# One pair of VectorE instructions for the row sums of both heads in an attention + mixture-of-experts kernel

## The chip, the cores and the metric

The kernel runs on one core of a Trainium2 chip. The metric is the device time of one execution in microseconds (us); lower is better. Before the change it is 1745.02 us, the median of three runs (1744.03 to 1747.92).

## The reference

Attention with a learned relative-position bias over 4 batches, 8 heads, 576 tokens and a head width of 64, and behind it eight dense experts (512 to 1024 to 512) over the 2304 tokens, each weighted by a gate that is normalised eight times over rows and columns. What the change touches is the softmax:

```python
scores = scale * np.matmul(q, k.transpose(0, 1, 3, 2))
...
scores = scores + bias.transpose(2, 0, 1)[None, :, :, :]
scores = scores - np.max(scores, axis=-1, keepdims=True)
attn = np.exp(scores)
attn = attn / (np.sum(attn, axis=-1, keepdims=True) + 1e-09)
return np.matmul(attn, v).astype(np.float32)
```

The experts then compute `out += P[:, e:e+1] * (np.maximum(x @ w1[e], 0) @ w2[e])` for each of the eight.

## The kernel before

A **unit** is one batch and two heads; there are 16. The 576 query rows of a head lie in tiles: four of 128 rows, and one in which the last 64 rows of both heads stand together. A **step** handles two tiles of one head (group `gi` 0 or 1, head `hh` 0 or 1) or the one shared tile (`gi` 2), so a unit has five steps: two pairs, of head 0 and head 1 over the same tokens, and a single one; 80 steps in all. For each tile of a step:

- TensorE multiplies the scores into a PSUM tile `s` (two of them).
- VectorE adds the bias and takes the row's extreme in one instruction (`st_max`, shown as CUSTOM_DVE_ANT_0 in the trace and ISA in the order, followed by a read of the accumulator); it writes the tile `sb` (six buffers) and a column of the statistics tile `st`.
- ScalarE takes the exponential in place, and the row sum with it (`st_exp`, followed by ACTIVATION_READ_ACCUMULATOR).
- VectorE adds 1e-9 to the sums and scales them (TENSOR_SCALAR), then takes the RECIPROCAL: `st_rcp`, one pair of instructions for each step.
- ScalarE multiplies the tile by the reciprocal into the high 16-bit half of `ah` (`st_hi`), and VectorE makes the low half from the rest (`st_lo`). `ah` has two buffers; in units 4 to 11 every third step uses a piece of `xc` as a third.
- A DMA transpose, issued from SyncE's queue, turns both halves into `aT` (three buffers for the steps with two tiles).
- Two steps later in program order `attend` multiplies by V, both heads of a pair in one group of 28 matmuls into `pv`.

While attention runs, TensorE also does the first expert, for blocks of tokens whose attention is finished ("pieces": `l<-xa`, `l<-xb`, `l<-xc` is its first layer, `l<-area` with 512 columns its second). They fill the gaps between scores and `pv`. The first units overlap with the computation of the bias and with the scaling of the first expert's weights.

The order on each engine is not the order of the code. A planner (`Plan`) records every operation with a cost, finds what depends on what from the memory regions, and picks for each engine, in simulated time, the ready operation of the highest priority and lowest number. A changed dependence or a changed place in the code can therefore move instructions all over the attention stage. Engines then run their lists strictly in order. The expert stage behind it (from 500 us on) has a planner run of its own.

The lines that matter:

```python
for n in range(NS + LAG + 1):
    ...
    if 0 < n <= NS:
        st_rcp(steps[n - 1])
    ...  # scores of step n + 1
    if n < NS:
        st_exp(steps[n])
    if n + 1 < NS:
        st_max(steps[n + 1])
    ...  # attend what is due
    if 0 < n <= NS:
        st_hi(s)      # s = steps[n - 1]
        st_lo(s)
```

Calls through the planner all have the line L210 in the trace, so the rows are told apart by their tiles.

Of the kernel before, what the change touches and what calls it, by code (L numbers as in the profile page):

```python
# [10 lines left out]
F32 = mybir.dt.float32  # L11
# [7 lines left out]
P = 128  # L19
# [251 lines left out]
def attention_sinkhorn_moe(ctx, tc, q, k, v, w1, b1, w2, wg, m1, m2, xm, xm4, xf, sel, out):  # L271
# [141 lines left out]
    with ExitStack() as actx:  # L413
# [4 lines left out]
        def places(name, bufs=1, space=None):  # L418
            kw = {} if space is None else {"space": space}
            p = atc.enter_context(tc.tile_pool(name=name, bufs=1, **kw))  # L420
            return Places(lambda k, n, size: p.tile([n, size], F32, name=k), bufs)
# [13 lines left out]
        nat, spl, uni, bst, wrk = places("nat", 4), places("spl"), places("uni", 2), places("bst", 2), places("wrk")  # L435
# [187 lines left out]
        def bias_step(between=()):  # L623

            i = bpos[0]
            bpos[0] += 1
            if between:
                if 0 < i <= NBLK:
                    bias_back(i - 1)
                for j, fn in enumerate(between):  # L630
                    fn()
                    if j == 0 and i < NBLK:
                        bias_front(i)
                return
            if i < NBLK:
                bias_front(i)
            if 0 < i <= NBLK:
                bias_back(i - 1)
# [145 lines left out]
        def b_tile(u, t, hh):  # L784
            if t in (2, 3):
                return U[u]["b", hh][:, t - 2, :]
            hp = units[u][1]
            return br[t][:, 2 * hp + hh, :] if t < 2 else br4[:, hp, :]
# [68 lines left out]
        def flush(n):  # L857
            while len(evacs) > n:
                evacs.pop(0)()
# [51 lines left out]
        def st_scores(s):  # L911
            u, gi, hh = s["key"]
            s["ps"] = []

            def one(t):
                with plan.as_one():
                    s["ps"].append(scores(u, t, hh))

            return [lambda t=t: one(t) for t in s["ts"]]

        def st_max(s):
            u, gi, hh = s["key"]
            st = wrk.tile([P, 4, 2], F32, name="st", tag="st", bufs=5)
            s["st"], s["sb"] = st, []
            for i, t in enumerate(s["ts"]):
                sb = wrk.tile([P, S], F32, name="sb", tag="sb", bufs=6)
                s["sb"].append(sb)
                vec.tensor_tensor_reduce(
                    out=sb,
                    in0=s["ps"][i][:, :S],  # L930
                    in1=b_tile(u, t, hh),
                    scale=nc8[:, 0:1],
                    scalar=3.0e38,
                    op0=ALU.add,
                    op1=ALU.min,
                    accum_out=st[:, 0, i : i + 1],
                )

        def st_exp(s):
            st = s["st"]  # L940
            for i, sb in enumerate(s["sb"]):
                act.activation(
                    sb, sb, AF.Exp, scale=-1.0, bias=st[:, 0, i : i + 1], accum_out=st[:, 2, i : i + 1]
                )

        def st_rcp(s):
            st, n = s["st"], len(s["ts"])
            vec.tensor_scalar(
                out=st[:, 3, :n], in0=st[:, 2, :n], scalar1=EPS, scalar2=TM14, op0=ALU.add, op1=ALU.mult
            )  # L950
            vec.reciprocal(out=st[:, 3, :n], in_=st[:, 3, :n])
# [3 lines left out]
        def st_hi(s):  # L955

            n, u = len(s["sb"]), s["key"][0]
            if NHP <= u < 3 * NHP:
                ahs[0] += 1
            if ahs[0] % 3 == 2 and u < 3 * NHP:  # L960
                ah = xc[:, 1, : 4 * S].rearrange("p (i s) -> p i s", i=2)
            else:
                ah = wrk.tile([P, 2, 2 * S], F16, name="ah", tag="ah", bufs=2)
            s["ah"] = ah[:, :n]
            for i, sb in enumerate(s["sb"]):
                act.activation(s["ah"][:, i, 0:S], sb, AF.Copy, scale=s["st"][:, 3, i : i + 1])

        def st_lo(s):
            n, ah = len(s["sb"]), s["ah"]
            s["aT"] = wrk.tile([P, 9 * n, P], F16, name="aT", tag="aT" if n == 2 else "aT4", bufs=3 if n == 2 else 1)  # L970
            for i, sb in enumerate(s["sb"]):
                vec.scalar_tensor_tensor(
                    out=ah[:, i, S:],
                    in0=sb,
                    scalar=s["st"][:, 3, i : i + 1],
                    in1=ah[:, i, 0:S],
                    op0=ALU.mult,
                    op1=ALU.subtract,
                )
            sync.dma_start_transpose(out=s["aT"], in_=ah.rearrange("p n s -> p (n s)"))  # L980
# [85 lines left out]
        def w_stage(j):  # L1066
            if j == -4:
                sync.dma_start(out=wgt, in_=wg.rearrange("(a p) e -> p a e", p=P))
            if j in (-4, -3):
                w_load(0, j + 4)  # L1070
                w_max(0, j + 4)
            if j == 0:
                for i in (2, 3):
                    w_load(0, i)
                for i in (2, 3):
                    w_max(0, i)
                for i in range(4):
                    w_load(1, i)
            if j == 5:
                w_scale(0)  # L1080
                for i in range(4):
                    w_cut(0, i)
            if j == 6:
                for i in range(4):
                    w_max(1, i)
                w_scale(1)
                for i in range(4):
                    w_cut(1, i)
# [7 lines left out]
        steps = []  # L1096
# [7 lines left out]
        NS = len(steps)  # L1104
# [26 lines left out]
        for fn in st_scores(steps[0]):  # L1131
            fn()
        st_max(steps[0])
        def fill(n):
            while xevac:
                xevac.pop(0)()
            for _ in range(n):
                if bpos[0] <= NBLK:
                    bias_step()

        W0 = 6
        for n in range(NS + LAG + 1):
            while xevac:
                xevac.pop(0)()
            if 0 < n <= NS:
                st_rcp(steps[n - 1])
            if n < W0:
                bias_step(st_scores(steps[n + 1]))
            elif n + 1 < NS:
                for fn in st_scores(steps[n + 1]):  # L1150
                    fn()
            if n < NS:
                st_exp(steps[n])
            if n + 1 < NS:
                st_max(steps[n + 1])
            if n < W0:
                fill(1)
            flush(0)
            for d in [d for d in due if d[0] <= n]:
                due.remove(d)  # L1160
                attend(*d[1:])
            if 0 < n <= NS:
                s = steps[n - 1]
                st_hi(s)
                st_lo(s)
                u, gi, hh = s["key"]
                groups.setdefault((u, gi), []).append(s)
                if gi == 2 or hh == 1:
                    due.append((n + LAG, u, gi, groups.pop((u, gi))))
            if n < W0:  # L1170
                fill(2)
            for fn in hooks.get(n, ()):
                fn()
            if n == W0 - 1:
                assert bpos[0] > NBLK
                hpl = Places(lambda k, n, size: area[:, 8192:])
            w_stage(n - W0)
            for _ in range(2 if n % 5 in (0, 2, 4) or n < 20 else 1):
                if pieces and n >= 13:
                    run_piece(*pieces.pop(0))  # L1180
            if n % 5 == 0 and pieces and pieces[0][1] is None and pieces[0][2] % 2:
                run_piece(*pieces.pop(0))
# [165 lines left out]
    for t in range(0, NT, 8):  # L1348
        ts = range(t, min(t + 8, NT))
# [625 lines left out]
def _build(nc, arrays):  # L1975
    args = []
    for name, a in arrays.items():
        args.append(nc.dram_tensor(name, a.shape, mybir.dt.from_np(a.dtype), kind="ExternalInput").ap())
    args.append(nc.dram_tensor("out_0_dram", (N, DM), F32, kind="ExternalOutput").ap())
    with tile.TileContext(nc) as tc:  # L1980
        attention_sinkhorn_moe(tc, *args)
# [14 lines left out]
```

## Time and profile before

| | |
|---|---|
| median of three runs | 1745.02 us |
| the profiled execution | 1748.49 us |
| its span, first to last instruction | 1746.7 us |
| attention stage | up to about 500 us |
| TensorE busy over the span | 1670.3 us (96%) |
| VectorE busy | 1437.3 us (82%) |
| ScalarE busy | 1073.4 us (61%) |

Busy shares over the whole span mix two stages. Behind 500 us the experts run, and TensorE is busy almost without a break. Ahead of it, all of the engines and the DMA queue are busy for some 85 to 95% of the time, and which one is waited for changes from stretch to stretch; so the stretches are read one by one. [...]

### The profile page before, as it was taken

The numbers are of one execution on the slowest core, as the hardware profiler recorded it, in microseconds if no ns is written. First come the engines' busy times: TensorE is split into PE (matmuls) and PEld (weight loads), VectorE is DVE, ScalarE is ACT, GpSimd is POOL, SyncE is SP. The second block draws the span as 40 slices with busy tenths as digits, with TensorE's granted clock in tenths as the row PEclk, the third lists the DMA queues.
The fourth block names the chain that finished last, engine by engine and source line by source line (L and its number), as shares of the span: only waits on it lengthen the run. The fifth ranks groups of instructions, "written<-read, shape, count | busy, mean of one in ns | idle before, by whom it ended". The sixth has DMA issues, their size and how long they took to land.

```text
span 1746.7 us, 40339 instructions
## 1 busy us (share of the span) xinstructions
PE 1670.3 (96%) x16596; PEld 1369.6 (78%) x16596; DVE 1437.3 (82%) x2619; ACT 1073.4 (61%) x1912; POOL 98.4 (6%) x137
## 2 busy tenths in 40 slices
PE   7887897989999999999999999999999999999998
PEld 4554564656575888888988898889888888888887
DVE  6898989888879999778878887988788878876666
ACT  7897888888867556446455545555554644443443
POOL 0012011111102310100000000000000000000000
PEclk9997899999999999999999999999999999999999
DMA  7869899999986346734564456456544743462321
GB/s 251 257 174 230 184 213 206 212 195 204 187 242 212 136 153 239 254 138 164 198 249 157 165 199 217 170 181 221 209 165 166 268 167 130 178 227 100 102 76 37
DMA packets 291965, 324.61 MB, mean 186 GB/s; under 512 B 183100, under 2 KB 217412, under 8 KB 286788
## 3 DMA queue, kind: packets, MB, share of 16 engines
q1 hardware_dynamic: 291780, 322.04, 61.3%
q8 instruction: 129, 2.11, 0.5%
q14 instruction: 56, 0.46, 0.1%
HBM read 191.43 MB, written 88.08 MB: 160 GB/s over the span
## 4 chain that ended last, share of the span: by engine, by line
PE 81%; DVE 9%; DMA 4%; ACT 3%; issue 2%; POOL 0%; SPq 0%; DVEq 0%; ACTq 0%; POOLq 0%
PE bankA L1607 18%; PE bankA L1627 14%; PE bankE L1627 9%; PE bankB L1627 9%; PE bankE L1607 9%; PE l L210 8%; PE bankB L1607 4%; PE s L210 4%; PE pv L210 3%; DMA aT<-ah 2%; ACT area L210 2%; DVE area L210 1%; DVE ah L210 1%; DVE sb L210 1%; PE bankB L374 1%
## 5 line engine op out<-in xcount | busy, mean ns | idle before, releaser
L1607 PEld LDWEIGHTS <-slot 128*128 128x128 f16 x5040 | 450.9, 98 | 51.2 <-issue 5.3
L1627 PEld LDWEIGHTS <-hA 128*128 128x128 f16 x2268 | 221.1, 98 | 26.5 <-DVE hA L1219 1.2
L210 PEld LDWEIGHTS <-area 128*128 128x128 f16 (+1 forms) x2477 | 154.7, 100 | 101.6 <-issue 33.3
L1607 PE MATMUL bankA<-xt,slot 128*128 128x256 f16 (+1 forms) x1680 | 186.1, 262 | 0.7 <-ACT u L1664 0.7
L1607 PE MATMUL bankE<-xt,slot 128*128 128x256 f16 (+1 forms) x1680 | 186.1, 262 | 0.3 <-DVE c L1219 0.3
L1652 ACT ACTIVATE hA<-c 128x512 f16<-128x512 f32 x189 | 118.3, 628 | 108.7 <-DVE c L1219 107.7
L1627 PEld LDWEIGHTS <-hS 128*128 128x128 f16 x1512 | 147.5, 98 | 20.2 <-DVE hS L1658 1.9
L1627 PEld LDWEIGHTS <-area 128*128 128x128 f16 x1512 | 147.7, 98 | 17.1
L1711 ACT COPY u<-bankA 128x512 f32<-128x512 f32 (+1 forms) x70 | 37.9, 541 | 177.4 <-PE bankA L1627 177.2
L1219 DVE SCALAR_TENSOR_TENSOR hA<-c,hA 128x512 f16<-128x512 f32 x189 | 128.4, 691 | 16.1 <-ACT hA L1652 14.1
L1664 ACT ACTIVATE u<-bankA 128x512 f32<-128x512 f32 x126 | 75.2, 597 | 79.0 <-PE bankA L1607 72.2
L210 PE MATMUL l<-area 128*128 128x512 f16 (+1 forms) x413 | 112.1, 390 | 4.9 <-ACT area L210 1.7
L210 ACT ACTIVATE sb<-sb,st 128x576 f32<-128x576 f32 x144 | 110.7, 770 | 7.5 <-DVE st L210 7.3
L1219 DVE SCALAR_TENSOR_TENSOR acc<-c,fs,acc 128x256 f32<-128x256 f32 x252 | 110.4, 480 | 2.1
L210 DVE SCALAR_TENSOR_TENSOR ah<-sb,st,ah 128x576 f16<-128x576 f32 x121 | 97.8, 833 | 15.1 <-ACT ah L210 15.0
L210 PE MATMUL s<-qkT 128*128 128x512 f16 (+3 forms) x560 | 84.0, 300 | 13.8 <-DVE st L210 13.2
L210 ACT ACTIVATE ah<-sb,st 128x576 f16<-128x576 f32 x121 | 89.4, 771 | 10.5 <-DMA aT<-ah 6.9
L1627 PE MATMUL bankA<-area,hS 128*128 128x256 f16 x756 | 88.9, 273 | 1.8 <-ACT hS L1652 1.0
L1627 PE MATMUL bankA<-area,hA 128*128 128x256 f16 x756 | 88.4, 273 | 1.0 <-DVE hA L1219 1.0
L1627 PE MATMUL bankB<-area,hA 128*128 128x256 f16 x756 | 88.3, 273 | 0.0
L1627 PE MATMUL bankB<-area 128*128 128x256 f16 x756 | 88.3, 273 | 0.0
L1627 PE MATMUL bankA<-area 128*128 128x256 f16 x756 | 88.3, 273 | 0.0
(248 smaller groups left out, 3173.1 us busy)
## 6 DMA issues: line engine op xcount, KB each, us to landing
sc_w<-stage SPq DMA_DIRECT2D x84, 512.0 KB
acc<-sc_y SPq DMA_DIRECT2D x102, 256.0 KB
area<-sc_w SPq DMA_DIRECT2D x48, 512.0 KB
sc_y<-acc SPq DMA_DIRECT2D x84, 256.0 KB
xt<-sc_t SPq DMA_DIRECT2D x20, 1024.0 KB
slot<-sc_w SPq DMA_DIRECT2D x36, 512.0 KB
bt<-sc_bias SPq DMA_DIRECT2D x26, 576.0 KB
raw<-in_moe_w_dram SPq DMA_DIRECT2D x28, 512.0 KB
```

Source lines behind the costliest of these rows:

```text
L210: self.plan.record(self.name, cost, lambda: fn(*args, **kw), ins, outs, move)
L374: pe.matmul(ps, w[:, a, ft * P : (ft + 1) * P], xs(xp, dt, p0, W), start=(dt == 0 and j == 0), stop=(dt == 3 and j == 2),)
L1219: vec.scalar_tensor_tensor(out=o, in0=x, scalar=s, in1=y, op0=op0, op1=op1)
L1607: pe.matmul(ps[:, jf * w : jf * w + w], t[:, a, c * 512 + f * P : c * 512 + f * P + P], x(xp, c), start=(first and jf == 0 and c == 0 and ...
L1627: pe.matmul(ps[:, j * 256 : j * 256 + 256], h[:, a, fc * w + j * P : fc * w + j * P + P], t[:, wp, fc * 256 : fc * 256 + 256], start=(firs ...
L1652: on_act(0.58, lambda: act.activation(h[:, 0, sl], x, AF.Relu if relu else AF.Copy), [r], wk)
L1664: on_act(0.55, lambda: act.activation(tmp[k], bank[b], f, scale=HS), [b], [k], 0)
L1711: on_act(0.27 * nt, lambda: act.copy(tmp[k][:, :n], bank[b][:, :n]), [b], [k], 0)
```

## The change

Both heads of a pair now share one statistics tile of four columns (three buffers, where there were five of two columns). After the first head's step no TENSOR_SCALAR and RECIPROCAL are issued; after the second's one pair of them works on all four columns. The high and low halves of the first head are made only then, ahead of the next step's `st_max` in the code, because that one reuses the first head's `sb` tiles. The steps with the shared tile stay as they were. `EPS` is 1e-9, and `TM14` a power of two.

```diff
+        stq = [None]
+
         def st_max(s):
             u, gi, hh = s["key"]
-            st = wrk.tile([P, 4, 2], F32, name="st", tag="st", bufs=5)
-            s["st"], s["sb"] = st, []
+            if hh == 0:
+                stq[0] = wrk.tile([P, 4, 4], F32, name="st", tag="st", bufs=3)
+            s["stats"] = stq[0]
+            s["st"], s["sb"] = stq[0][:, :, 2 * hh : 2 * hh + 2], []
+            st = s["st"]
...
         def st_rcp(s):
-            st, n = s["st"], len(s["ts"])
+            st, n = s["stats"], 4 if s["key"][1] < 2 else 1
             vec.tensor_scalar(
                 out=st[:, 3, :n], in0=st[:, 2, :n], scalar1=EPS, scalar2=TM14, op0=ALU.add, op1=ALU.mult
             )
...
         for n in range(NS + LAG + 1):
             while xevac:
                 xevac.pop(0)()
-            if 0 < n <= NS:
+            ended = steps[n - 1]["key"] if 0 < n <= NS else None
+            waits = ended is not None and ended[1] < 2 and ended[2] == 0
+            if ended and not waits:
                 st_rcp(steps[n - 1])
...
             if n < NS:
                 st_exp(steps[n])
+            if ended and ended[2] == 1:
+                st_hi(steps[n - 2])
+                st_lo(steps[n - 2])
             if n + 1 < NS:
                 st_max(steps[n + 1])
...
             if 0 < n <= NS:
                 s = steps[n - 1]
-                st_hi(s)
-                st_lo(s)
+                if not waits:
+                    st_hi(s)
+                    st_lo(s)
```

**On VectorE**, in a late unit, before: `st_132` and `st_135` are the statistics of the two heads of a first pair, `st_139` and `st_143` those of the second pair; ISA is the score-plus-bias instruction into `sb`.

```order
L210 TENSOR_SCALAR st_132<-st_132 128x2
L210 ISA sb_134,st_139<-s_117,bt_122,sms 128x576
L210 ISA st_139 128x1
L210 RECIPROCAL st_132<-st_132 128x2
L210 SCALAR_TENSOR_TENSOR ah_144<-sb_136,st_146,ah_144 128x576
L210 TENSOR_TENSOR area<-l_1_115,area 128x512
L210 ISA sb_136,st_139<-s_119,bt_122,sms 128x576
...
L210 COPY qkT_127<-l_1_115 128x1024
L210 TENSOR_SCALAR st_135<-st_135 128x2
L210 RECIPROCAL st_135<-st_135 128x2
L210 SCALAR_TENSOR_TENSOR ah_142<-sb_137,st_132,ah_142 128x576
```

Now, at the same kind of place: `st_132` holds both heads of the first pair, `st_138` both of the second.

```order
L210 TENSOR_SCALAR st_132<-st_132 128x4
L210 RECIPROCAL st_132<-st_132 128x4
L210 SCALAR_TENSOR_TENSOR ah_141<-sb_136,st_132,ah_141 128x576
L210 SCALAR_TENSOR_TENSOR xc<-pv_112,xc 128x256
L210 ISA sb_136,st_138<-s_117,bt_124,sms 128x576
L210 ISA st_138 128x1
L210 SCALAR_TENSOR_TENSOR ah_141<-sb_139,st_132,ah_141 128x576
L210 SCALAR_TENSOR_TENSOR ah_142<-sb_140,st_132,ah_142 128x576
L210 ISA sb_139,st_138<-s_119,bt_124,sms 128x576
...
L210 SCALAR_TENSOR_TENSOR ah_142<-sb_133,st_132,ah_142 128x576
```

Before, the two heads' sums are treated apart, with the next pair's ISA between them; now one pair of instructions stands ahead of the low halves of both heads, and the ISA of the next pair's second head goes into an `sb` that the low half just before has set free.

**On ScalarE**, before (rows `sb<-sb` are exponentials, rows `ah<-sb` and `xc<-sb` high halves):

```order
L210 ACTIVATE ah_142<-sb_137,st_132 128x576
L210 ACTIVATE ah_142<-sb_140,st_132 128x576
L210 COPY qkT_127<-l_0_113 128x1024
L210 ACTIVATE sb_134,st_139<-sb_134,st_139 128x576
L210 ACTIVATE sb_136,st_139<-sb_136,st_139 128x576
L210 COPY qkT_127<-l_0_113 128x2x128
L210 ACTIVATE xb<-pv_112 128x256
L210 ACTIVATE xc<-sb_141,st_135 128x576
L210 ACTIVATE xc<-sb_133,st_135 128x576
```

And now, a little later in the list:

```order
L210 ACTIVATE sb_140,st_132<-sb_140,st_132 128x576
L210 ACTIVATE sb_133,st_132<-sb_133,st_132 128x576
L210 ACTIVATE qk_126<-nat_121,sms 128x9x64
L210 ACTIVATE sb_134,st_138<-sb_134,st_138 128x576
L210 ACTIVATE sb_135,st_138<-sb_135,st_138 128x576
L210 ACTIVATE ah_141<-sb_136,st_132 128x576
L210 ACTIVATE ah_141<-sb_139,st_132 128x576
L210 ACTIVATE xc<-sb_140,st_132 128x576
L210 ACTIVATE xc<-sb_133,st_132 128x576
```

Before, two high halves of one head alternate with exponentials; now the four of a pair stand in a row, behind the exponentials of the next step.

**On SyncE's queue**, before (`aT` is the transposed tile, `vnat`, `nat` and `bt` are loads for later units):

```order
L210 DMA_TRANSPOSE aT_125<-ah_144 128x18x128
L210 DMA nat_120<-in_k_dram 128x576
L210 DMA_TRANSPOSE aT_138<-ah_142 128x18x128
L210 DMA nat_121<-in_q_dram 128x576
L210 DMA_TRANSPOSE aT_0_118<-xc 128x9x128
L210 DMA bt_122<-sc_bias 128x1152
```

Now:

```order
L210 DMA nat_121<-in_q_dram 128x576
L210 DMA_TRANSPOSE aT_125<-ah_142 128x18x128
L210 DMA_TRANSPOSE aT_137<-ah_141 128x18x128
L210 DMA_TRANSPOSE aT_0_118<-xc 128x9x128
L210 DMA bt_122<-sc_bias 128x1152
```

The transposes of the two heads have moved together; the loads that stood between them stand ahead or behind.

## Rows read from the trace of the kernel before

**Rows 1.** Stretches: length, busy PE, PEld, DVE, ACT, POOL; PEclk, DMA share, GB/s.
```profile
100.00:150.00 50.00, 45.68 (x675) 28.90 (x674) 45.77 (x100) 46.45 (x93) 11.14 (x20) 1.00 0.78 192
150.00:205.00 55.00, 38.33 (x331) 22.59 (x329) 52.47 (x120) 41.45 (x79) 3.89 (x9) 0.75 1.02 230
205.00:275.00 70.00, 68.17 (x649) 43.20 (x644) 60.46 (x139) 59.31 (x121) 9.93 (x13) 0.98 0.96 201
275.00:310.00 35.00, 23.62 (x252) 14.20 (x252) 31.81 (x75) 28.19 (x59) 4.95 (x10) 0.82 0.94 203
310.00:500.00 190.00, 181.42 (x1821) 118.59 (x1820) 156.39 (x361) 156.28 (x321) 23.04 (x35) 0.98 0.97 201
```

**Rows 2.** Groups of TensorE, 275 to 310 us: busy us, mean ns | idle before, releaser.
```profile
L210 PE MATMUL pv<-aT,vs 128*64 128x256 f16 (+3 forms) x168 | 12.8, 298 | 3.4 <-DMA aT<-xc 2.3 <-DVE xb L210 0.6 <-DVE st L210 0.5
L210 PE MATMUL s<-qkT 128*128 128x512 f16 (+2 forms) x65 | 10.0, 296 | 5.2 <-DVE st L210 5.0
```

**Rows 3.** The same view, 310 to 345 us: the first expert's layer.
```profile
L210 PE MATMUL l<-xb,area 128*128 128x256 f16 x111 | 13.5, 273 | 0.0
```

**Rows 4.** Waits, 150 to 205 us: total us, times, longest.
```profile
PE s L210 <- DVE st L210: 8.5, 7, 2.6
PE pv L210 <- DMA aT<-ah: 4.0, 2, 2.3
```

**Rows 5.** Stretches of 5 us, columns as in rows 1.
```profile
280.00:285.00 5.00, 1.30 (x8) 0.54 (x7) 4.96 (x12) 5.00 (x11) 1.07 (x3) 0.85 0.85 157
285.00:290.00 5.00, 4.55 (x37) 3.02 (x38) 4.12 (x9) 1.85 (x5) 0.00 (x0) 0.50 0.96 221
```

**Rows 6.** Tile st, whole span: count, ns min/median/max, first and last start.
```profile
L210 DVE TENSOR_SCALAR st<-st x80: 131/159/506, 81.6 to 482.7; 128x2 f32<-128x2 f32 x64, 128x1 f32<-128x1 f32 x16
L210 DVE RECIPROCAL st<-st x80: 141/163/167, 83.5 to 482.9; 128x2 f32<-128x2 f32 x64, 128x1 f32<-128x1 f32 x16
```

**Rows 7.** Timeline of VectorE: start, us, operation.
```profile
333.72 0.17 DVE L210 TENSOR_SCALAR st<-st 128x2 f32<-128x2 f32 x1
333.79 0.81 DVE L210 CUSTOM_DVE_ANT_0 sb<-s,bt,sms 128x576 f32<-128x576 f32 x1
334.53 0.16 DVE L210 RECIPROCAL st<-st 128x2 f32<-128x2 f32 x1
334.61 0.80 DVE L210 SCALAR_TENSOR_TENSOR ah<-sb,st,ah 128x576 f16<-128x576 f32 x1
...
338.72 0.16 DVE L210 TENSOR_SCALAR st<-st 128x2 f32<-128x2 f32 x1
338.92 0.17 DVE L210 RECIPROCAL st<-st 128x2 f32<-128x2 f32 x1
339.00 1.54 DVE L210 SCALAR_TENSOR_TENSOR xc<-sb,st,xc 128x576 f16<-128x576 f32 x2
```

**Rows 8.** Tile st in 150 to 205, in 275 to 310 and in 310 to 500 us.
```profile
L210 DVE RECIPROCAL st<-st x10: 141/156/160, 154.6 to 202.9; 128x2 f32<-128x2 f32 x8, 128x1 f32<-128x1 f32 x2
...
L210 DVE RECIPROCAL st<-st x9: 151/160/167, 275.9 to 308.7; 128x2 f32<-128x2 f32 x7, 128x1 f32<-128x1 f32 x2
...
L210 DVE RECIPROCAL st<-st x40: 151/165/167, 313.3 to 482.9; 128x2 f32<-128x2 f32 x32, 128x1 f32<-128x1 f32 x8
```

**Rows 9.** Tile st, whole span: exponentials, high and low halves.
```profile
L210 ACT ACTIVATE sb<-sb,st x144: 758/767/837, 69.9 to 481.8; 128x576 f32<-128x576 f32 x144
L210 ACT ACTIVATION_READ_ACCUMULATOR sb<-sb,st x144: 185/191/263, 70.5 to 482.5; 128x1 f32 x144
L210 ACT ACTIVATE ah<-sb,st x121: 755/769/826, 85.9 to 489.6; 128x576 f16<-128x576 f32 x121
L210 DVE SCALAR_TENSOR_TENSOR ah<-sb,st,ah x121: 797/814/1254, 88.0 to 490.4; 128x576 f16<-128x576 f32 x121
```

**Rows 10.** Tile aT, 60 to 500 us: the transposes on SyncE's queue.
```profile
L210 SPq DMA_TRANSPOSE aT<-ah x67: 1271/3094/5702, 90.1 to 491.5; - x67
```

**Rows 11.** The chain of waits, 145 to 165 us: start, us, what.
```profile
152.40 8.72 DMA aT<-ah
```

## The prediction

> **What bounds the kernel now.** I began with the table of stretches [rows 1]. From 500 us on TensorE has hardly a gap and the change leaves that part's code as it is, so only the attention stage can move. In it two stretches differ from the rest. From 205 to 275 us TensorE is busy 68.2 of 70 us and from 310 to 500 us 181.4 of 190; from 150 to 205 us it is busy only 38.3 of 55 us at a mean clock of 0.75, and from 275 to 310 us 23.6 of 35 at 0.82. In these two VectorE is busy 52.5 of 55 and 31.8 of 35, the highest share of any compute engine: there it sets the pace.
>
> Next, the groups of TensorE in the second of them [rows 2]: before scores it stood idle 5.2 us (5.0 of it until VectorE had read the score tile), before `pv` 3.4 us, 2.3 of that for a transpose. The costly groups of the first expert that fill such gaps elsewhere (111 matmuls of one layer alone in the next 35 us, with 0.0 idle before them [rows 3]) are missing: no block was finished yet. From 150 to 205 us the waits say the same: 8.5 us of scores for VectorE, 4.0 us of `pv` for transposes [rows 4]. [...]
>
> [...]
>
> **The removed instructions.** There are 80 TENSOR_SCALAR and 80 RECIPROCAL on `st`, 64 of each on two columns [rows 6]. 64 heads make 32 pairs, so 32 of each go: 64 instructions. By their durations (medians 159 and 163 ns) that is 32 x 0.322 = 10.3 us. But the timeline shows that a duration is not what the queue gives up [rows 7]: a TENSOR_SCALAR starts at 333.72 and the next instruction 0.07 us later, a RECIPROCAL at 334.53 and its successor 0.08 later. Only where the RECIPROCAL directly follows and needs the result is it more: 338.72 to 338.92 to 339.00, 0.28 for both. In the order of instructions 37 of the 80 reciprocals directly follow their TENSOR_SCALAR before, and 26 of 48 now. So VectorE gives up 37 x 0.28 + 43 x 0.15 = 16.8 us before and 26 x 0.28 + 22 x 0.15 = 10.6 now: 6.2 us less, 0.19 per pair. Four columns have no row; two and one lie in one band (141 to 167 ns for the RECIPROCAL [rows 6]), so I cost four as two.
>
> [...]
>
> How much of it counts? Only pairs in the two stretches where VectorE sets the pace: 8 and 7 reciprocals on two columns [rows 8], one per head, so 7.5 pairs. 7.5 x 0.19 = 1.4 us. Where TensorE is full the cover is TensorE's own queue, and the gain there is nothing; without that cover it would be the other 24.5 x 0.19 = 4.7 us.
>
> **The added wait.** The one TENSOR_SCALAR now waits for the exponentials of the second head. Behind it on VectorE stand the RECIPROCAL, four low halves and the score instructions of the next pair's second head, which wait for `sb` tiles that these free; on ScalarE stand four high halves in a row. Is this loop too long? By [rows 7, 9]: the pair of instructions 0.36 us; two high halves and then the second low half, 0.77 + 0.77 + 0.81 = 2.35; two score instructions of 0.81 each, 1.62; the exponential and its read, 0.77 + 0.19 = 0.96. Sum 5.3 us a pair, without the handing over between engines. The pace is far slower: 32 two-column reciprocals in 190 us [rows 8] are 16 pairs, or 8 units of 23.8 us, and two loops are 10.6. So the six `sb` suffice and I cost this wait by itself at 0. If an engine's queue delays every turn of it by more than 6 us, that cover is gone.
>
> What is late next is `pv`. It needs both heads' transposes. The order shows them moved together: of 80 transposes 19 directly follow another one before, 37 now. SyncE's queue takes 3.09 us for one [rows 10]. The second head's low halves are done two low halves (1.5 us) after the first's, so its transpose stands for 3.09 - 1.5 = 1.6 us behind the first; and since its own high and low halves now come behind the first head's, another 1.5 us can be added. Bounds for one `pv`: 0 (what the planner puts in front covers it) to 3.1 us. Nor does a reason exclude a small gain: a load that stood between the two no longer delays the second one. No row here times that; I bound it by the shortest transpose, 1.3 us [rows 10]. Between -1.3 and 3.1 I take 1.6, the part that the queue itself forces.
>
> Where does it count? Where `pv` already waits for a transpose and nothing stands in front: twice from 150 to 205 us and once from 275 to 310 [rows 2, 4]. One of these is the transpose that took 8.72 us to land from 152.40 [rows 11]; that one was slow because of other traffic (the weights' loads), not for its neighbour, so I leave it out. 2 x 1.6 = 3.2 us. In the full stretches the first expert's matmuls cover it.
>
> **Sum.** -1.4 + 3.2 = +1.8 us. The profiled execution took 1748.49 us, 1.7 above its span and 3.5 above the median of 1745.02; with the same difference the median becomes about 1747.
>
> **Rivals.** *VectorE sets the pace all along, and fewer instructions are simply faster.* For it: its share is 95% and 91% in the slow stretches, and ScalarE and the DMA queue are not far behind TensorE elsewhere, so each unit may tighten. Against it: 0.0 idle of TensorE before the filling matmuls [rows 3], and a busy 95% there. Price: all 6.2 us by starts, which gives 1739; by durations 10.3, which gives 1735.
>
> *The late pair of transposes stops TensorE and drops its clock.* For it: the waits and the 0.50 behind the pause [rows 2, 4, 5]; two stretches in which nothing fills. Against it: the planner charges transfers and shifts `pv` accordingly. It decides once `pv` comes more than about 2 us later than what stands in front of it lasts. Price: three waits x 3.1 = 9.3 us, and one more stretch of 5 us at half clock, 2.5 us of lost work, less the 1.4 gained: +10.4, so 1755. With the clock lost at all three it is +15.4, so 1760.
>
> *It doesn't do what it says*: the planner only reshuffles, VectorE's saved time turns into VectorE's idle time and the transposes are covered. Then nothing moves: 1745.
>
> **How the numbers follow.** A measurement of this kernel can tell about 0.2%, 3.5 us, from no change. Forecast (1747, its own range 1742 to 1750): 0.35. Faster rival (up to 1741.5, around 1739): 0.32. Slower rival (from 1749, around 1755): 0.27. No effect (1745): 0.06. The forecast lies 0.29 within 3.5 us of the median and 0.06 above it. So faster 0.32, same 0.29 + 0.06 = 0.35, slower 0.06 + 0.27 = 0.33. The range leaves out a tenth on each side, about a third of either rival: what the faster one gives beyond its price by durations, and the slower one between its two prices and above: 1735 to 1758.
>
> **What would show it.** VectorE with 64 instructions fewer, 48 of each kind, four columns at about 160 ns; its busy time down by some 10 us but its place in the stage by less. Transposes in twos on SyncE's queue. The wait of `pv` for transposes, 6.3 us in the two slow stretches, up by about 3. The first expert stage starting within 4 us of 500. I am wrong if the waits for score tiles (8.5 and 5.0 us) shrink by more than 3 us, which is the faster rival, or if TensorE's clock in either slow stretch falls further, which is the slower one.

## The result, and the profile after

The changed kernel takes 1754.66 us (median of five; 1751.19 to 1754.94 without one disturbed execution of 8830.24 us) against 1745.02 before (median of five, 1742.55 to 1747.92): ratio 1.0051, 95% interval 1.0036 to 1.0066, so about 9 us slower. The range of the prediction, 1735 to 1758, holds it; its central 1747 does not. 1755 was the price of the rival in which the late pair of transposes stops TensorE.

The profiled execution of the changed kernel took 1751.19 us, the shortest of its runs, with a span of 1749.4; that of before (1748.49) was longer than any of those five runs, with a span of 1746.7. So the two profiles differ by 2.7 us only, and show less of the loss than the medians. The engines' row of the page: busy us, share, instructions.

```profile
PE 1671.4 (96%) x16596; PEld 1370.1 (78%) x16596; DVE 1428.4 (82%) x2555; ACT 1075.3 (61%) x1912; POOL 98.3 (6%) x137
```

VectorE has 64 instructions fewer (x2619 before) and 8.9 us less work (1437.3 before). Now the stretches of [rows 1], same columns, with the first half of the first one by itself in front:

```profile
100.00:125.00 25.00, 20.94 (x247) 12.40 (x244) 20.84 (x45) 19.30 (x38) 5.55 (x8) 0.88 0.80 190
...
150.00:205.00 55.00, 36.17 (x305) 21.87 (x303) 53.17 (x114) 42.32 (x78) 5.08 (x8) 0.78 0.96 234
...
275.00:310.00 35.00, 24.70 (x254) 14.56 (x252) 30.87 (x72) 31.64 (x66) 6.76 (x10) 0.90 1.09 221
310.00:500.00 190.00, 179.51 (x1789) 117.17 (x1790) 156.08 (x337) 157.96 (x320) 21.85 (x35) 0.98 0.98 203
```

The first 25 us of it before the change:

```profile
100.00:125.00 25.00, 21.75 (x288) 12.71 (x287) 24.40 (x56) 23.51 (x47) 4.77 (x8) 1.00 0.81 200
```

From 310 to 500 us VectorE's work hardly fell (156.39 before, 156.08 now), and TensorE does less (181.42, 179.51): work has moved to a later time. From 100 to 125 us, where the bias is made while the first heads run, VectorE had been busy 24.40 of 25 us and ScalarE 23.51. Now they are busy 20.84 and 19.30, and TensorE's granted clock (PEclk, as a share of full speed) is 0.88 there, where it was 1.00. This is a place that the prediction did not look at: it read 100 to 150 us as one row.

The tile `st` in the whole span now (count: ns min/median/max, first and last start):

```profile
L210 ACT ACTIVATE sb<-sb,st x144: 757/770/809, 68.4 to 484.1; 128x576 f32<-128x576 f32 x144
...
L210 DVE TENSOR_SCALAR st<-st x48: 109/158/259, 87.9 to 485.0; 128x4 f32<-128x4 f32 x32, 128x1 f32<-128x1 f32 x16
L210 DVE RECIPROCAL st<-st x48: 140/166/179, 88.3 to 485.2; 128x4 f32<-128x4 f32 x32, 128x1 f32<-128x1 f32 x16
...
who waited for it (us, times):
  DVE ah L210: 22.9, 21
...
  ACT sb L210: 16.7, 27
```

And the same two of the view before:

```profile
  DVE ah L210: 15.0, 16
  ACT sb L210: 7.3, 11
```

`ACT sb` is ScalarE standing still until VectorE has the maxima of a score tile, in front of an exponential: 27 times now, 11 before. `DVE ah` is VectorE standing still in front of a low half: 22.9 us, 15.0 before. Each engine now stands before the other more often. The first exponential starts 1.5 us earlier than in [rows 9] (68.4 for 69.9), the last 2.3 later (484.1 for 481.8).

The instructions on four columns took as long as those on two, within 3 ns: medians of 158 and 166 ns for the 48 now, 32 of them on four columns, and of 159 and 163 ns for the 80 before [rows 6]. VectorE's timeline, to be held against [rows 7] (the next instruction again starts 0.07 us later):

```profile
330.97 0.15 DVE L210 TENSOR_SCALAR st<-st 128x4 f32<-128x4 f32 x1
331.04 0.80 DVE L210 CUSTOM_DVE_ANT_0 sb<-s,br,sms 128x576 f32<-128x576 f32 x1
```

The waits of TensorE from 150 to 205 us and from 275 to 310 (us, times, longest):

```profile
PE pv L210 <- DMA aT<-ah: 8.7, 4, 2.7
PE s L210 <- DVE st L210: 7.5, 9, 1.3
...
PE s L210 <- DVE st L210: 4.7, 6, 1.9
PE pv L210 <- DMA aT<-ah: 2.1, 2, 1.1
```

In the first, `pv` waits for transposes 8.7 us, where it was 4.0 [rows 4]; the waits for score tiles fell by 1.0 only. SyncE's queue shows what has changed (start, us; `area<-in_moe_w_dram` are loads of the first expert's weights). After:

```profile
152.73 5.44 SPq L210 DMA_TRANSPOSE aT<-ah  x2
158.22 4.08 SPq L210 DMA_DIRECT2D area<-in_moe_w_dram  x6
162.40 11.14 SPq L210 DMA_TRANSPOSE aT<-ah  x2
```

Before:

```profile
145.94 3.38 SPq L210 DMA_TRANSPOSE aT<-ah  x1
...
150.74 1.33 SPq L210 DMA_DIRECT2D area<-in_moe_w_dram  x2
152.40 5.28 SPq L210 DMA_TRANSPOSE aT<-ah  x1
157.79 2.75 SPq L210 DMA_DIRECT2D area<-in_moe_w_dram  x4
160.64 8.71 SPq L210 DMA_TRANSPOSE aT<-ah  x2
```

These are the transposes of the third pair and, in the last row, of the fourth (the order of steps begins with the first pairs of units 0 to 3). Before, the third pair's first head went out alone at 145.94, its partner at 152.40, with two weight loads between them and four behind. Now both go out from 152.73 on: the first has waited for the second. All six loads have come behind them, and so ahead of the fourth pair's two transposes, which stood together before as well: these start 1.8 us later and take 11.14 us, where they took 8.71. ScalarE shows the wait too, with the third pair's four high halves in one row, where the first head's had been made at 134.39 and 142.81 us before:

```profile
148.22 2.79 ACT L210 ACTIVATE ah<-sb,st 128x576 f16<-128x576 f32 x4
```

TensorE's timeline has the price, the third and, in the last two rows, the fourth pair's `pv` with the idle time ahead of them:

```profile
162.12 2.47 PE L210 MATMUL pv<-aT,xb 128*64 128x256 f16 x27 [1.87 <-DMA aT<-ah]
172.78 0.37 PE L210 MATMUL pv<-aT,xb 128*64 128x256 f16 x1 [2.75 <-DMA aT<-ah]
175.50 3.42 PE L210 MATMUL pv<-aT,xb 128*64 128x256 f16 x27 [2.34 <-DMA aT<-ah]
```

Before:

```profile
161.16 3.42 PE L210 MATMUL pv<-aT,xb 128*64 128x256 f16 x27 [2.28 <-DMA aT<-ah]
172.15 3.48 PE L210 MATMUL pv<-aT,xb 128*64 128x256 f16 x28
```

The third pair's wait did not grow (2.28 us before, 1.87 now). The fourth pair's `pv` waits 5.1 us, and had not waited.

### The profile page after: what moved, and what is told of

Read it like the earlier page. It is cut to its first block, busy times and chain, and to the rows that moved or that the text cites. A ratio compares the mean times of both kernels' runs of the same rounds, so it can differ in the third digit from the quotient of the medians.

```text
span 1749.4 us, 40251 instructions
## 1 busy us (share of the span) xinstructions
PE 1671.4 (96%) x16596; PEld 1370.1 (78%) x16596; DVE 1428.4 (82%) x2555; ACT 1075.3 (61%) x1912; POOL 98.3 (6%) x137
## 4 chain that ended last, share of the span: by engine, by line
PE 81%; DVE 8%; DMA 4%; ACT 3%; issue 2%; SPq 0%; POOL 0%; DVEq 0%; ACTq 0%; POOLq 0%
PE bankA L1618 18%; PE bankA L1638 14%; PE bankE L1638 9%; PE bankB L1638 9%; PE bankE L1618 9%; PE l L210 8%; PE s L210 4%; PE bankB L1618 4%; PE pv L210 3%; ACT area L210 2%; DVE area L210 1%; DVE sb L210 1%; DMA aT<-ah 1%; DVE ah L210 1%; PE bankB L374 1%
## 5 line engine op out<-in xcount | busy, mean ns | idle before, releaser
L1638 PEld LDWEIGHTS <-area 128*128 128x128 f16 x1512 | 147.7, 98 | 17.1
L210 ACT ACTIVATE sb<-sb,st 128x576 f32<-128x576 f32 x144 | 110.8, 771 | 17.2 <-DVE st L210 16.7
L210 DVE SCALAR_TENSOR_TENSOR ah<-sb,st,ah 128x576 f16<-128x576 f32 x121 | 97.4, 832 | 23.0 <-ACT ah L210 22.9
```

Of the source, the lines that this page charges most:

```text
L210: self.plan.record(self.name, cost, lambda: fn(*args, **kw), ins, outs, move)
L1638: pe.matmul(ps[:, j * 256 : j * 256 + 256], h[:, a, fc * w + j * P : fc * w + j * P + P], t[:, wp, fc * 256 : fc * 256 + 256], start=(firs ...
```

## The experiments

All times are compared with the kernel before, timed in turn on the same chip; its median was 1745.44 us beside e1 to e4, 1744.51 beside e5 to e8 and 1744.15 beside e9 to e12.

**The theory: the wait itself costs.** Head 0's tiles are done, but VectorE and ScalarE may not work on them until head 1's exponentials are through; their order has gaps, and `pv` gets both transposes late. (Theory A in the expectations is the last part alone: late transposes stop TensorE behind 150 us. A' is that the first head's wait costs.) **Rival 1:** the pairing only shuffles a planned order, and any shuffle moves the time this much. **Rival 2:** the loss sits only in the first pairs, where nothing fills. **Rival 3:** the saved instructions do gain, and hide part of a larger loss.

**e1_late and e2_early** split the change by place. Both go through one function that says which pairs are merged; a pair that isn't keeps its two instructions per head and its place as before.

```
+        def paired(key):
+            u, gi, hh = key
+            return gi < 2 and (u >= 4 or gi > 0)      # e1_late
+            return gi < 2 and u < 4 and gi == 0       # e2_early
...
-            waits = ended is not None and ended[1] < 2 and ended[2] == 0
+            waits = ended is not None and ended[2] == 0 and paired(ended)
```

> Heads are paired only from the second row group (gi 1 of units 0 to 3) on; the four pairs that run beside the bias computation keep one pair of instructions per head. Theory A (late transposes stop TensorE where pv waits for them, 150 to 205 and 275 to 310 us): all such places stay, so the loss stays, ratio to before 1.003 to 1.006. Rival B (the loss is made before 150 us, where the planner reorders scores and bias steps): the loss goes, 0.999 to 1.002.

Measured: 1749.25 us, ratio 1.0025 (1.0012 to 1.0039).

> The complement: only the four pairs beside the bias computation are paired. Theory A: 0.999 to 1.001. Rival B: 1.003 to 1.006, and the stretch up to 150 us late by 4 us or more against before.

Measured: 1755.32 us, ratio 1.0058 (1.0045 to 1.0070). Four pairs of 32 do as much as the whole change, and the other 28 still do half of it. Theory A expected next to nothing of e2 and is refuted as the whole account; rival B is right for e2 and not for e1, which lies between the two forecasts. Both kernels have five statistics tiles where the changed one has three, so a lack of these tiles is not what costs them. The two parts don't add up (0.83% against 0.51%). In e2's waits from 140 to 205 us, the loss shows in another place than in the changed kernel:

```profile
PE l L210 <- DVE sms L210: 8.9, 3, 6.7
...
PE pv L210 <- DMA aT<-ah: 1.7, 1, 1.7
```

Here it is not `pv` that is late but the scales of the weights (`sms`), a short chain on VectorE whose next part comes, in this order, only behind two low halves: one wait of 6.7 us. So which wait ends last is chosen by the order.

**e3_wait_only** keeps the waiting and gives the saving back: each head has its own two instructions again, behind the second head's exponentials.

```
 def st_rcp(s):
-            st, n = s["stats"], 4 if s["key"][1] < 2 else 1
+            st, n = s["st"], len(s["ts"])
...
             if ended and not waits:
+                if ended[2] == 1:
+                    st_rcp(steps[n - 2])
                 st_rcp(steps[n - 1])
```

> The first head waits for the second as in the change, but each head keeps its own TENSOR_SCALAR and RECIPROCAL, so no instruction is saved. If the wait and the new order are the whole cost and the saved instructions bring little (my forecast: 1.4 us): 1.005 to 1.007. If the saved instructions count in full (6 us): 1.008 to 1.010. If the merged instruction itself were what costs: 1.000 to 1.002.

Measured: 1756.60 us, ratio 1.0069 (1.0053 to 1.0085). With nothing saved, the wait and its new order cost as much as the whole change or more (the two intervals overlap). `pv` waits 7.2 us for transposes from 140 to 205 us:

```profile
PE pv L210 <- DMA aT<-ah: 7.2, 4, 2.3
```

**e4_rcp_only** is the other half: the kernel before, no waiting, with half of the small instructions gone. It leaves out adding 1e-9 and the scaling by 2^-14, so the reciprocal is of the bare sums.

```
-            vec.tensor_scalar(
-                out=st[:, 3, :n], in0=st[:, 2, :n], scalar1=EPS, scalar2=TM14, op0=ALU.add, op1=ALU.mult
-            )
-            vec.reciprocal(out=st[:, 3, :n], in_=st[:, 3, :n])
+            vec.reciprocal(out=st[:, 3, :n], in_=st[:, 2, :n])
```

> The kernel before, with the addition of 1e-9 and the scaling by 2^-14 left out: 80 VectorE instructions fewer and no wait added. By the starts in the timeline some 10 us less of VectorE's queue. If VectorE sets the pace all along: 0.994 to 0.996. If it does so only in the two slow stretches (a quarter of the pairs): -2 to -3 us, 0.998 to 0.999. If nothing waits for it: 1.000.

Measured: 1745.84 us, ratio 1.0005 (0.9994 to 1.0017). 80 instructions of VectorE less, 16 more than the change takes away, show no gain; the interval leaves 0.06%, about 1 us. But e4 has an order of its own too, and a new order alone moved this kernel by 0.9988 and 1.0006 (e5 and e6 below). So, as an estimate from these, up to some 3 us could hide in it; 6 or 10 us hardly. That leaves rival 3 little room. Its profile has no TENSOR_SCALAR on the tile, and the reciprocals as before:

```profile
L210 DVE RECIPROCAL st<-st x80: 143/160/173, 79.7 to 479.6; 128x2 f32<-128x2 f32 x64, 128x1 f32<-128x1 f32 x16
```

**e5 to e8** test rival 1. A small change of a planner's number shuffles the order without touching the work, on the kernel before (e5, e6) and on the changed one (e7, e8): the latency from VectorE to TensorE, or the cost of an instruction of one or two columns.

```
-        ("dve", "pe"): 0.26,       # e5_reshuffle_before, e7_reshuffle_after
+        ("dve", "pe"): 0.27,
...
-            return 0.08            # e6_reshuffle_before2, e8_reshuffle_after2
+            return 0.1
```

> The kernel before with one number of the planner changed that has nothing to do with the pairing (the hand-over from VectorE to TensorE costs 0.27 and not 0.26): only the order on the engines moves. Theory A' (the wait of the first head is what costs): 0.998 to 1.002. Rival (any new order loses against one that happens to be good): 1.003 to 1.007.

Measured: 1742.81 us, ratio 0.9988 (0.9979 to 0.9997).

> The kernel before with the planner's cost of small VectorE instructions at 0.10 and not 0.08: another order. Theory A': 0.998 to 1.002. Rival: 1.003 to 1.007.

Measured: 1745.48 us, ratio 1.0006 (0.9995 to 1.0017).

> The changed kernel with the planner's hand-over cost at 0.27. Theory A': the loss stays whatever the order, 1.003 to 1.007. Rival: the ratio spreads as the reshuffled kernels without pairing do, and may be 0.999 to 1.002.

Measured: 1755.92 us, ratio 1.0058 (1.0043 to 1.0074).

> The changed kernel with the planner's cost of small VectorE instructions at 0.10. Theory A': 1.003 to 1.007, with TensorE's first pv some 4 us later against the stage's start than without pairing. Rival: anywhere from 0.999 to 1.007.

Measured: 1749.40 us, ratio 1.0028 (1.0016 to 1.0039). The orders of one kernel lie up to 0.3% apart, so rival 1 has a part in the size: the changed kernel is 1.0051, 1.0058 or 1.0028 by order, the one before 1, 0.9988 or 1.0006. But in all three orders the merged kernel is slower than in any of the three without, though e8 lies just below what A' expected and its first `pv` is not late as A' had it.

**e9_from_unit4** merges from unit 4 on only, and leaves the bias stage and the first blocks as before; **e10_from_unit4_reshuffled** is the same in the order that was best for the kernel before.

```
+            return gi < 2 and u >= 4
...
-        ("dve", "pe"): 0.26,       # e10 only
+        ("dve", "pe"): 0.27,
```

> Heads are paired only from unit 4 on, which starts at about 205 us, behind the bias computation and the weight loads. If the wait costs only where the first units meet bias and weight loads, and the saved instructions gain 2 to 3 us behind 300 us as the traces with pairing show: 0.998 to 1.000. If the wait costs in every unit: 1.002 to 1.004.

Measured: 1748.94 us, ratio 1.0027 (1.0016 to 1.0038).

> Paired from unit 4 on, with the planner's hand-over from VectorE to TensorE at 0.27, which alone gave 0.9988. If both gains add: 0.996 to 0.998. If pairing from unit 4 on gains nothing: 0.998 to 1.000; if it costs: above 1.001.

Measured: 1748.29 us, ratio 1.0025 (1.0015 to 1.0036). With the first four units untouched the early loss is gone. ScalarE's evacuation of the first two `pv` (its copy out of PSUM; start, us) in e9:

```profile
134.60 0.39 ACT L210 ACTIVATE xa<-pv 128x256 f16<-128x256 f32 x1 [0.38 <-PE pv L210]
147.14 0.40 ACT L210 ACTIVATE xa<-pv 128x256 f16<-128x256 f32 x1
```

In the changed kernel:

```profile
137.74 0.38 ACT L210 ACTIVATE xa<-pv 128x256 f16<-128x256 f32 x1 [0.34 <-PE pv L210]
152.48 0.36 ACT L210 ACTIVATE xa<-pv 128x256 f16<-128x256 f32 x1
```

12.5 us lie between the two in e9 (and before: 135.58 and 148.12), 14.7 in the changed kernel. But a loss of 0.25% stays: rival 2 doesn't hold either.

**e11_weights_later** asks whether the long transposes from 152 us on are slow because of the weight loads beside them. It moves the loads of the second layer's weights three steps on; **e12_weights_later_before** is the same move on the kernel before.

```
 def w_stage(j):
...
             if j == 0:
...
                 for i in (2, 3):
                     w_max(0, i)
+            if j == 3:
                 for i in range(4):
                     w_load(1, i)
```

> The changed kernel with the loads of the first expert's second weights asked for three steps later, so that two weight loads and not six go out between the second and the third two transposes. If the late transposes cost because they stand behind these loads: the waits of pv for transposes from 140 to 205 us fall from 8.7 to 4 us or less, and the ratio from 1.005 to 1.002 or 1.003. If they cost because both heads come late: waits and ratio stay.

Measured: 1750.80 us, ratio 1.0036 (1.0023 to 1.0049).

> The control: the kernel before with the same three steps' delay of the weight loads. Its transposes are not collected; if the loads matter only for those, 0.999 to 1.001. If the delay is good or bad for itself, this shows by how much.

Measured: 1747.51 us, ratio 1.0019 (1.0010 to 1.0028). Where nothing is paired the move costs a little, more than was expected. In the paired kernel the waits of `pv` from 140 to 205 us add up to what they were (8.7 us in the changed kernel):

```profile
PE pv L210 <- DMA aT<-ah: 8.6, 5, 2.4
```

But they are not the same waits. The `pv` of the fourth pair and of the next one in e11, and SyncE's queue:

```profile
170.54 3.42 PE L210 MATMUL pv<-aT,xb 128*64 128x256 f16 x27 [1.27 <-DMA aT<-ah]
180.89 0.37 PE L210 MATMUL pv<-aT,vs 128*64 128x256 f16 x1 [2.04 <-DMA aT<-ah]
183.62 3.42 PE L210 MATMUL pv<-aT,vs 128*64 128x256 f16 x27 [2.36 <-DMA aT<-ah]
...
168.65 2.25 SPq L210 DMA_DIRECT2D area<-in_moe_w_dram  x4
171.26 10.40 SPq L210 DMA_TRANSPOSE aT<-ah  x2
```

The fourth pair, whose transposes now have two weight loads ahead of them and not six, waits 1.27 us, where it waited 5.1. The next pair, which doesn't wait in the changed kernel, waits 4.4 us, and its two transposes stand right behind the four loads that were moved. So in the paired kernel the wait goes where the loads go, and only the sum stays; in e12, with the loads moved and nothing paired, the same two `pv` wait 0.49 and 0.15 us. In all of these rows `pv` waits most where two transposes go out together behind four or six loads (4.4 us and 5.1); but before the change two behind four loads (160.64 us) made no wait, so the loads are not the whole cause either. A third buffer for `ah` or eight `sb` instead of six, which might loosen the wait, were not tried.

All runs together, with the time from the first exponential's start to the second `pv` evacuation in each profile, and how often ScalarE waited for maxima in the whole span:

| kernel | merged | first exponential to second `pv` | ScalarE's waits for maxima | ratio |
|---|---|---|---|---|
| before | none | 78.3 us | 7.3 us, 11 | 1 |
| e5, e6 | none | 77.8, 76.3 | 4.8, 8; 7.7, 10 | 0.9988, 1.0006 |
| e4 | none | 80.9 | 4.7, 8 | 1.0005 |
| e12 | none | 78.5 | 6.0, 10 | 1.0019 |
| e1, e9, e10 | later ones | 78.4, 78.3, 78.3 | 11.3, 20; 10.3, 20; 9.1, 17 | 1.0025, 1.0027, 1.0025 |
| e2 | first four | 82.4 | 6.5, 10 | 1.0058 |
| after, e7 | all | 84.1, 82.7 | 16.7, 27; 16.1, 27 | 1.0051, 1.0058 |
| e11, e8 | all | 81.5, 76.8 | 11.0, 21; 15.1, 24 | 1.0036, 1.0028 |
| e3 | all, no saving | 82.1 | 10.8, 16 | 1.0069 |

Two losses can be told apart. Where the first pairs wait, the second `pv` comes 81.5 to 84.1 us after the first exponential instead of 76.3 to 80.9, and these are the kernels with 1.0036 and more; e8, whose order avoids it, has 1.0028. With one profile for each kernel, and e4 at 80.9 without a loss, this is a tendency. Where only the later pairs wait, 0.25 to 0.27% is lost with the early stage as before, and ScalarE waits for maxima about twice as often. This second loss is close to e12's 1.0019, with nothing paired; that e1, e8, e9 and e10 agree in it speaks for the pairing. No version of the change beats the kernel before; the best run is e5, the kernel before in another order (0.9988).

## Why the prediction was half right

**What bounds the kernel** was read rightly for the slow stretches: 150 to 205 us is where `pv` waits. (That all engines are busy for 85 to 95% ahead of 500 us is too even: by [rows 1] TensorE is at 67 to 97% and ScalarE at 75 to 93%.) It was read too coarsely ahead of them. The row of 100 to 150 us in [rows 1] has VectorE at 45.77 of 50 us, which hides that it and ScalarE are full in its first half (24.40 and 23.51 of 25). There the halves of a head are what ScalarE does between two pieces of the bias. Before, the last half of the first pair and the first of the second stand in one row of ScalarE's timeline, just behind VectorE's RECIPROCAL for the second pair's first head:

```profile
102.12 0.14 DVE L210 RECIPROCAL st<-st 128x2 f32<-128x2 f32 x1
...
102.35 1.45 ACT L210 ACTIVATE ah<-sb,st 128x576 f16<-128x576 f32 x2
...
110.91 0.76 ACT L210 ACTIVATE ah<-sb,st 128x576 f16<-128x576 f32 x1
```

And after, where the first pair's halves are all made and the second's may not begin until both heads' sums are there:

```profile
108.69 0.60 ACT L210 ACTIVATE area<-pv 128x512 f16<-128x512 f32 x1 [2.60 <-PE s L210]
...
114.25 0.17 DVE L210 RECIPROCAL st<-st 128x4 f32<-128x4 f32 x1
...
117.16 0.81 ACT L210 ACTIVATE ah<-sb,st 128x576 f16<-128x576 f32 x1
```

ScalarE stands still for 2.60 us ahead of 108.69, and the second pair's first half is made at 117.16 us instead of about 103, its next at 121.50 instead of 110.91. In the two profiles the first `pv` is evacuated 65.7 us after the first exponential before and 69.4 after; that is 3.7 of the 5.9 us by which the second `pv` is later. The sum had no term for it. e8, which merges all pairs and has 62.1 there, shows that another order can avoid it; e4, with nothing merged and 68.8, that an order without any wait can have it. So it is a loss of this order, to which the wait gave the occasion; the runs don't part the two further.

**The removed instructions (-1.4 us)** came out as written in count (64 fewer, 48 of each) and in length (medians of 158 and 166 ns). Their worth is not measured that finely: e4 shows no gain, but orders alone differ by more than 1.4 us (0.08%). It speaks against 6.2 and 10.3, on which the faster rival stood, because e4 takes away some 10 us of VectorE's queue by start times and more by durations, and the time did not move. It doesn't choose between the two ways of reading; the starts 0.07 us apart do.

**The added wait (0)** is the step that failed. I priced it as a loop of 5.3 us against a pace of 23.8 us a unit and found it hidden. That asks whether the loop can keep up, not what it does to the order. e3 (1.0069) is this term and its order without the saving. In e9, with 1.0027, the bias stage and the first `pv` are as before, and most of its merged pairs lie where the first expert's matmuls fill, where I had the wait covered. What the traces show there is the pair of waits from `st`: maxima late for exponentials, halves late for each other. How these become 4 to 5 us at the end stays open. In the profiles of e1, e9 and e10 TensorE turns from attention to the gate at 498.81, 496.74 and 498.52 us, no later than before (499.71), and the gate's part described in the last section takes 15.9, 15.8 and 17.4 us, where it took 14.9. So no profile shows this loss inside attention, and whether the wait makes it there or in what follows is not shown.

**The late transposes (+3.2 us)** were the right mechanism in the right stretch, but on the wrong `pv` and without what gives them their size. In the two slow stretches `pv` waits 10.8 us for them (8.7 and 2.1) where I had 6.3 and expected 3 more. The two waits to which the 3.2 us were added did not grow: the one behind the third pair's in the first stretch was 1.77 us and one of 1.77 is there now, the one in the second was 2.3 and is 2.1. The growth is the 5.1 us of the fourth pair, which had not waited. Its transposes stand together in both kernels; now six weight loads and not four stand ahead of them, because the third pair's first transpose waits for the second head (145.94 became 152.73). The prediction left the weight loads out as other traffic (that they slowed the transpose of 8.72 us was my estimate and is not shown), and in e11 the wait went where they went: 1.27 us for the fourth pair, 4.4 for the next.

**The slower rival** (+10.4, 1755) gave the time almost exactly, for reasons that hold in part: three late `pv` were priced at 9.3 us, and 4.7 was found. Its second half, a further fall of the clock in the slow stretches, did not come: the granted clock is 0.78 from 150 to 205 us and 0.90 from 275 to 310, where it was 0.75 and 0.82; it fell from 100 to 125 us instead (1.00 to 0.88). The condition of about 2 us and the 2.5 us for one more stretch at half clock were my estimates; no run shows either, and from 150 to 205 us the clock was not lower with 8.7 us of waits for transposes than with 4.0. The rest of its price stands for the losses of the added wait. So the time agrees with it better than its reasons do, and it is partly luck that the range, which took in this rival, holds the result: the sum had +1.8 us for a loss of about 9.

**The signs I named**: `pv`'s waits up by about 3 (4.5), score tiles' waits not shrunk by more than 3 (1.0 and 0.3), the expert stage within 4 us of 500 us (last `pv` evacuated at 502.24, 499.82 before). All three fit a small loss, and the profile, a short execution, showed just that; the runs showed more than three times as much.

## What to carry to other kernels

Merging two tiny instructions of two steps makes the earlier step's result wait for the later one: price the wait, not the instructions. Here taking out 80 instructions of 0.16 us showed no gain, and every kernel in which heads waited, whatever its order, was 0.25 to 0.7% slower. When a loop is shorter than the pace, ask also which fill work it takes away from an engine that is full; read the stretches finely enough to see where one is. Ask what else stands in the queue of a transfer that is held back: here six loads that came behind it, from 158.22 us on, were ahead of the next one, which took 11.14 us. And where an order is planned, run a shuffled one of both kernels: it tells a loss of the edit from a loss of its order.

## What the runs showed of the chip beyond that

At the end of attention TensorE turns to the gate, matmuls of 8 columns, the first of them in the changed kernel at 502.13 us:

```profile
502.13 1.36 PE L1286 MATMUL bankS<-wgs,xa 128*128 128x8 f16 x48
...
516.70 0.27 PE L1265 MATMUL bankS<-ident,fs 128*1 128x128 f32 x1
```

Though TensorE is busy 3.89 to 4.00 of 4 us there, the granted clock falls; the stretches of the changed kernel, columns as in [rows 1]:

```profile
500.00:504.00 4.00, 4.00 (x115) 3.56 (x114) 1.25 (x4) 1.28 (x3) 0.00 (x0) 1.00 1.00 289
504.00:508.00 4.00, 4.00 (x75) 3.29 (x72) 4.00 (x8) 1.73 (x4) 0.00 (x0) 0.58 1.02 424
```

And of e4, where it lasts longer:

```profile
500.00:504.00 4.00, 3.89 (x104) 3.49 (x102) 4.00 (x8) 3.23 (x6) 0.00 (x0) 0.50 1.02 422
504.00:508.00 4.00, 4.00 (x45) 3.00 (x43) 3.68 (x10) 3.18 (x7) 0.00 (x0) 0.50 0.42 174
```

From the first of these matmuls to `bankS<-ident` it is 14.6 us in the changed kernel, 14.9 before and 17.1 in e4; over all fourteen profiles it is 14.6 to 17.4. So a profile can win or lose up to 3 us there, whatever attention did: e4's attention ended 3.1 us earlier than before's (496.71 us), and its span is 0.7 longer (1747.4). With one profile for each kernel it is not shown whether the order or the single execution decides.
